# Reordering the first two batches of a linear-attention and bilinear-FFN kernel: kv before transposes in batch 0, x as full-row products in batch 1

## The chip, the cores and the metric

The kernel runs on one core of one Trainium2 chip. The metric is the device time of one execution in microseconds (us). One execution of each kernel was also taken with the hardware profiler. The profiled spans are about 1.8 us shorter than the times, because the span runs from the first to the last instruction.

In this text "PE" is TensorE, the matrix engine. "PEld" is its weight loads, "DVE" is VectorE, "ACT" is ScalarE and "POOL" is GpSimd. "SP" is the engine that issues the stores and the DMA transposes.

## The reference

```python
# q, k, v: (8 batches, 8 heads, 576 tokens, 64); g_norm: (64,)
kv  = einsum('bhsd,bhse->bhde', k, v)          # a 64x64 matrix per head
out = einsum('bhsd,bhde->bhse', q, kv)
rms = sqrt(mean(out * out, axis=-1) + 1e-6)
x   = (out / rms * g_norm)                     # as (4608 tokens, 512)
y   = ((x @ w_a) * (x @ w_b)) @ w_out          # 512 -> 1536 -> 512
```

## The kernel before

Heads are handled in pairs, so that two of 64 columns fill 128 partitions (the copies of `qT` in the trace are 128x576). For one pair the steps are as follows:

- transposes of q (`qtr`), then a DVE copy out of PSUM (`qtr_out`);
- kv (`kv1`), then a copy of it (`kv1_out`);
- x = q kv (`px`);
- squares on ACT (`psq`);
- sums of squares by a product with a block matrix of ones, then the reciprocal root on ACT (`pss`);
- the scaled result `xt` on DVE (`pst`).

`dummy` products of zeros fill PE's waits. The FFN works on strips of 512 tokens. Strip 0 needs batch 0 only, and strip 1 needs batch 1 too. Batches 0 and 1 are loaded and computed at the start. Later batches are computed between the FFN's products ("slots").

```python
        def px(self, p, i0):                 # x as four 64x64 products
            for h in range(2):
                for j in range(2):
                    r = slice(j * D, (j + 1) * D)
                    nc.tensor.matmul(P[r, i0 + h, 0:HF], lhsT=self.kvs[r, p, :],
                        rhs=self.qT[r, p, h * HF : (h + 1) * HF], start=True, stop=True)

        def x(self, p, i0):                  # x as two full-row products, kv block-diagonal
            for h in range(2):
                nc.tensor.matmul(P[:, i0 + h, 0:HF], lhsT=kvb[self.b % 2][:, p, :],
                    rhs=self.qT[:, p, h * HF : (h + 1) * HF], start=True, stop=True)
    # ... (cut) batch 0; banks of PSUM: X, SS = (4, 0), 6
    A.kv1(0, 3)
    A.kv1_out(0, 3, nc.vector.tensor_copy)
    for p in range(NP - 1):
        i = X[p % 2]
        A.qtr(p + 1, 2 + (p + 1) % 2)
        A.qtr_out(p + 1, 2 + (p + 1) % 2)
        if p:
            A.pst(p - 1, X[(p - 1) % 2])
        A.px(p, i)
        A.psq(p, i)
        # ... (cut) g_col at p == 0
        dummy(1, 2 + p % 2)
        A.kv1(p + 1, 2 + p % 2)
        dummy(1, 7)
        A.pss(p, SS)
        A.kv1_out(p + 1, 2 + p % 2, nc.vector.tensor_copy)
        if p < NP - 2:
            dummy(1, 2 + (p + 1) % 2)
    A.px(3, X[1])
    # ... (cut) squares of pair 3 in two halves, pst(2); the first two FFN units:
    u0.first((0, 1))                         # chunks 0 and 1 of w_a, then of w_b
    A.pss(3, SS, (0,))
    A.pst(3, X[1], (0,))
    u0.first((2,))                           # chunk 2: the "upper" weights
    A.pss(3, SS, (1,))
    A.pst(3, X[1], (1,))
    u1.first((0, 1, 2))
    u0.rest((3,))
```

## Time and profile before

| | before |
|---|---|
| median of 4 runs (range) | 323.93 us (323.7 to 324.06) |
| span of the profiled run | 322.1 us |
| PE busy | 97% of the span |
| granted PE clock | 1.000 |

The page of the kernel before, parts 1 and 4. Part 1 gives busy time per engine, and part 4 gives the chain of work that ended last, as shares of the span:

```profile
PE 314.1 (97%) x1922; PEld 151.0 (47%) x1957; DVE 124.3 (39%) x215; ACT 124.7 (39%) x212; POOL 60.3 (19%) x82
...
PE 87%; DMA 9%; POOL 1%; issue 1%; DVE 0%; ACT 0%; POOLq 0%; ACTq 0%
```

PE is the bound. Of the 9% of DMA in the chain, all but the last store (0.6%) lies in the first 33 us, where the first q and the weights arrive.

The view of waits of the kernel before, engine PE (who waited <- for whom: us in total, times, longest):

```profile
PE P L303 <- DVE eps_t L318: 1.2, 1, 1.2
PE P L137 <- issue: 0.5, 2, 0.3
PE P L161 <- DVE kvs L155: 0.3, 1, 0.3
PE P L278 <- issue: 0.3, 2, 0.2
PE P L234 <- DVE xt L202: 0.3, 1, 0.3
PE P L161 <- DVE qt L344: 0.2, 1, 0.2
```

PE's listed waits are 2.8 us in all, so almost everything left to save is work on PE itself.

The timeline of the kernel before, engine PE (start, us taken, what, count, and in brackets the idle time before it and what ended it). L137 is kv, L161 the transposes, L175 x as 64x64 products, L188 the sums, L234 the FFN's first layer, L278 its second:

```profile
7.12 0.38 PE L137 MATMUL P<-vt,kt 96*64 96x64 bf16 x12
7.82 0.45 PE L161 MATMUL P<-ident,qt 96*64 96x96 bf16 x12 [0.32 <-DVE kvs L155]
8.20 0.43 PE L175 MATMUL P<-qT,kvs 64*64 64x288 bf16 x4
...
14.42 0.43 PE L175 MATMUL P<-qT,kvs 64*64 64x288 bf16 x4
...
16.25 0.38 PE L234 MATMUL P<-xt,wa_t 128*128 128x512 bf16 x1 [0.31 <-DVE xt L202]
16.46 0.38 PE L234 MATMUL P<-xt,wb_t 128*128 128x512 bf16 x1
...
44.41 0.41 PE L188 MATMUL P<-sq,ones 128*128 128x288 bf16 x2
44.75 0.43 PE L175 MATMUL P<-qT,kvs 64*64 64x288 bf16 x4
45.11 0.45 PE L161 MATMUL P<-ident,qt 96*64 96x96 bf16 x12
```

At 7.82 us the transposes of pair 1 stand behind a DVE copy. At 14.42 us x of the last pair of batch 0 starts. Read distances between starts, because the durations of products overlap (the two at 16.25 and 16.46 us take 0.38 us each).

### The profile page before, as it was taken

How to read it: one execution, taken by the hardware profiler on the slowest of the kernel's cores; microseconds unless marked ns; L12 is line 12 of the kernel's file. 1: busy time of each engine (PE TensorE's matmuls, PEld its weight loads, DVE VectorE, ACT ScalarE, POOL GpSimd, SP SyncE). 2: the span in 40 equal slices, each digit the busy share in tenths (PEclk: the TensorE clock that was granted, in tenths of full speed). 3: DMA queues.
4: the chain of work that ended last, by engine and by line, in shares of the span. 5: the costliest groups of instructions: out<-in, count | busy, mean ns of one | idle time of the engine just before them, and what ended most of it. 6: DMA issues, size and time to landing. Idle time of an engine off the chain costs nothing.

```text
span 322.1 us, 4818 instructions
## 1 busy us (share of the span) xinstructions
PE 314.1 (97%) x1922; PEld 151.0 (47%) x1957; DVE 124.3 (39%) x215; ACT 124.7 (39%) x212; POOL 60.3 (19%) x82
## 2 busy tenths in 40 slices
PE   7999999999999999999999999999999999999995
PEld 3444454444444444444444445444444444444443
DVE  3544334344234433453244423532354243314421
ACT  3643245453335423552355325433453233123310
POOL 8855870330041240500050000000000000000000
PEclk9999999999999999999999999999999999999999
DMA  8999999795359899894598150003000200020002
GB/s 180 197 196 199 196 209 211 127 149 99 90 98 162 123 160 226 72 159 95 140 98 124 67 131 7 2 33 99 2 0 2 98 33 0 32 86 16 2 33 98
DMA packets 70043, 32.61 MB, mean 101 GB/s; under 512 B 43652, under 2 KB 65540, under 8 KB 70020
## 3 DMA queue, kind: packets, MB, share of 16 engines
q0 software_dynamic: 49712, 18.44, 48.5%
q1 hardware_dynamic: 19952, 13.50, 16.2%
q10 hardware_dynamic: 356, 0.36, 0.4%
q8 instruction: 15, 0.25, 0.3%
q14 instruction: 8, 0.07, 0.1%
HBM read 37.75 MB, written 12.98 MB: 157 GB/s over the span
## 4 chain that ended last, share of the span: by engine, by line
PE 87%; DMA 9%; POOL 1%; issue 1%; DVE 0%; ACT 0%; POOLq 0%; ACTq 0%
PE P L234 52%; PE P L278 28%; DMA wa_t<-in_moe_w_a_dram 5%; PE P L188 2%; PE P L214 2%; PE P L137 2%; DMA qt<-in_q_dram 2%; DMA wo_t<-in_moe_w_out_dram 1%; DMA out_dram<-osb 1%; PE P L161 0%; PE P L175 0%; POOL wb_t L108 0%; POOL wa_t L107 0%; POOL wa_t L331 0%; DVE osb L293 0%
## 5 line engine op out<-in xcount | busy, mean ns | idle before, releaser
L250 DVE TENSOR_TENSOR ab<-P,asb 128x512 bf16<-128x512 f32 x108 | 74.5, 692 | 124.0 <-PE P L234 123.1
L234 PE MATMUL P<-xt,wa_t 128*128 128x512 bf16 x425 | 111.4, 379 | 1.0 <-DVE xt L202 0.3
L234 PE MATMUL P<-xt,wb_t 128*128 128x512 bf16 x417 | 109.7, 379 | 0.4
L278 PE MATMUL P<-wo_t,ab 128*128 128x512 bf16 (+1 forms) x433 | 97.0, 373 | 0.8 <-issue 0.3
L248 ACT CAST asb<-P 128x512 bf16<-128x512 f32 x108 | 63.0, 585 | 81.5 <-PE P L234 80.0
L234 PEld LDWEIGHTS <-wb_t 128*128 128x128 bf16 x432 | 42.2, 98 | 51.2 <-DMA wb_t<-in_moe_w_b_dram 0.3
L278 PEld LDWEIGHTS <-ab 128*128 128x128 bf16 x444 | 43.0, 98 | 45.8 <-issue 0.2
L234 PEld LDWEIGHTS <-wa_t 128*128 128x128 bf16 x432 | 41.7, 98 | 44.5 <-DMA wa_t<-in_moe_w_a_dram 0.3
L202 DVE SCALAR_TENSOR_TENSOR xt<-P,g_col,rs 128x288 bf16<-128x288 f32 x64 | 30.2, 513 | 25.4 <-ACT rs L192 25.4
L192 ACT ACTIVATE rs<-P,eps_t 128x576 f32<-128x576 f32 (+1 forms) x33 | 24.0, 727 | 23.1 <-PE P L188 19.1
L291 ACT COPY osb<-P 128x512 f32<-128x512 f32 x17 | 10.0, 585 | 48.9 <-PE P L278 47.1
L184 ACT ACTIVATE sq<-P 128x576 bf16<-128x576 f32 x31 | 20.2, 650 | 20.3 <-PE P L214 18.0
L293 DVE COPY osb<-P 128x512 f32<-128x512 f32 x18 | 12.4, 691 | 32.5 <-PE P L278 32.5
L119 POOL DMA_DIRECT2D qs<-in_q_dram x12 | 19.6, 1633 | 1.7 <-issue 1.7
L116 POOL COPY gate<-qT 1x1 bf16<-1x1 bf16 x5 | 0.9, 176 | 92.7 <-DMA qT<-qs 92.7
L188 PE MATMUL P<-sq,ones 128*128 128x288 bf16 x64 | 13.2, 286 | 0.0
L214 PE MATMUL P<-qT,kvb 128*128 128x288 bf16 x48 | 10.0, 286 | 0.0
L188 PEld LDWEIGHTS <-ones 128*128 128x128 bf16 x64 | 6.3, 98 | 7.2
L96 POOL DMA_DIRECT2D vt<-in_v_dram x13 | 9.1, 702 | 1.1 <-DMA wo_t<-in_moe_w_out_dram 0.7
L96 POOL DMA_DIRECT2D kt<-in_k_dram x13 | 9.2, 709 | 0.0
L137 PE MATMUL P<-vt,kt 96*64 96x64 bf16 x384 | 8.6, 197 | 0.5 <-issue 0.5
L137 PEld LDWEIGHTS <-kt 96*64 96x64 bf16 x384 | 7.2, 112 | 3.6 <-issue 3.2
(43 smaller groups left out, 65.4 us busy)
## 6 DMA issues: line engine op xcount, KB each, us to landing
out_dram<-osb SPq DMA_DIRECT2D x23, 256.0 KB, 2.0
qs<-in_q_dram POOLq DMA_DIRECT2D x12, 288.0 KB, 6.7
kt<-in_k_dram POOLq DMA_DIRECT2D x6, 576.0 KB, 8.8
vt<-in_v_dram POOLq DMA_DIRECT2D x6, 576.0 KB, 11.1
out_dram<-osb SPq DMA_DIRECT2D x13, 128.0 KB, 2.3
wo_t<-in_moe_w_out_dram POOLq DMA_DIRECT2D x12, 128.0 KB, 6.3
wa_t<-in_moe_w_a_dram POOLq DMA_DIRECT2D x5, 256.0 KB, 9.2
wb_t<-in_moe_w_b_dram POOLq DMA_DIRECT2D x5, 256.0 KB, 9.8
```

The costliest lines, as they stand in the source:

```text
L96: nc.gpsimd.dma_start(out=t[:, hs, :, :], in_=src[b, hs].rearrange("h (t c) d -> t h c d", c=EC))
L119: nc.gpsimd.dma_start(out=d[:, hs, :], in_=q[b, hs].rearrange("h t d -> t h d"))
L137: nc.tensor.matmul(o[j * D : (j + 1) * D, :], lhsT=kt[self.b % NB][:, 2 * p + j, c, :], rhs=vt[self.b % NB][:, 2 * p + j, c, :], start=(c ...
L184: nc.scalar.activation(sq[p % 3], P[:, i0 : i0 + 2, 0:HF], AF.Square)
L188: nc.tensor.matmul(P[:, i0 + h, 0:HF], lhsT=ones, rhs=sq[p % 3][:, h, :], start=True, stop=True)
L192: nc.scalar.activation(rs[p % 3][:, h0:h1, :], P[:, i0 + h0 : i0 + h1, 0:HF], AF.Abs_reciprocal_sqrt, bias=eps_t,)
L202: nc.vector.scalar_tensor_tensor(out=xt[p][:, t0 : t0 + HF], in0=P[:, x0 + h, 0:HF], scalar=g_col, in1=rs[p % 3][:, h, :], op0=ALU.mult, o ...
L214: nc.tensor.matmul(P[:, i0 + h, 0:HF], lhsT=kvb[self.b % 2][:, p, :], rhs=self.qT[:, p, h * HF : (h + 1) * HF], start=True, stop=True,)
L234: nc.tensor.matmul(self.a if w is wa_t else self.b, lhsT=w[:, kc, self.fc * 128 : (self.fc + 1) * 128], rhs=xt[kc][:, t0 : t0 + STRIP], st ...
L248: nc.scalar.copy(self.t, self.a)
L250: nc.vector.tensor_mul(abt[self.s % 2][self.fc], self.b, self.t)
L278: nc.tensor.matmul(P[:, i, e0:e1], lhsT=abt[s % 2][fc][:, g * 128 : (g + 1) * 128], rhs=wo_t[:, fc, e0:e1], start=(fc == 0), stop=(fc == F ...
```

## The change

Its intent in batch 0 is to run kv as soon as its pair has landed, then the sums of squares of the pair before, then the next transposes, then x. The dummies stand in two places only, one product before the transposes and two behind x. Pair 0's kv uses a PSUM bank that the next transposes don't need. In batch 1, x runs as two full-row products (`x`) instead of four 64x64 ones (`px`), which needs two ACT copies per pair to fill the block diagonal.

```diff
-        def kv_out(self, src):
+        def kv_out(self, ps, src):
             for j in range(2):
                 r = slice(j * D, (j + 1) * D)
-                nc.scalar.copy(kvb[self.b % 2][r, :, r], src[r])
+                nc.scalar.copy(kvb[self.b % 2][r, ps, r], src[r])
 # ... (cut) batch 0: the loop shown above is replaced by
+    A.kv1(0, SS)
+    A.kv1_out(0, SS, nc.vector.tensor_copy)
+    A.qtr(1, 3)
+    A.qtr_out(1, 3)
+    A.px(0, X[0])
+    A.psq(0, X[0])
+    for p in range(1, NP):
+        i = X[p % 2]
+        A.kv1(p, 3 - p % 2)
+        A.kv1_out(p, 3 - p % 2, nc.vector.tensor_copy)
+        A.pss(p - 1, SS)
+        if p < NP - 1:
+            # ... (cut) g_col at p == 1
+            dummy(1, 2 + p % 2)
+            A.qtr(p + 1, 3 - p % 2)
+            A.qtr_out(p + 1, 3 - p % 2)
+            A.pst(p - 1, X[(p - 1) % 2])
+            A.px(p, i)
+            A.psq(p, i)
+            dummy(2, 2 + p % 2)
 # ... (cut) batch 1
-            A.px(n - 1, X[(n - 1) % 2])
+            A.x(n - 1, X[(n - 1) % 2])
 # ... (cut)
-            A.kv1_out(n, 2, nc.scalar.copy)
+            A.kv_out(n, P[:, 2, STRIP - D :])
 # ... (cut) the later batches' call of kv_out, with slice(0, NP) for all pairs
```

More of the change, by code (lines that the diff above doesn't have):

```diff
@@ L351 @@
     dummy(4, 7)
-    A.kv1(0, 3)
-    A.kv1_out(0, 3, nc.vector.tensor_copy)
-    for p in range(NP - 1):
-        i = X[p % 2]
-        A.qtr(p + 1, 2 + (p + 1) % 2)
-        A.qtr_out(p + 1, 2 + (p + 1) % 2)
-        if p:
-            A.pst(p - 1, X[(p - 1) % 2])
-        A.px(p, i)
-        A.psq(p, i)
-        if p == 0:
-            nc.tensor.matmul(P[:, 1, 0:1], lhsT=g_row, rhs=one, start=True, stop=True)
-            nc.vector.tensor_copy(g_col, P[:, 1, 0:1])
-        dummy(1, 2 + p % 2)
-        A.kv1(p + 1, 2 + p % 2)
-        dummy(1, 7)
-        A.pss(p, SS)
-        A.kv1_out(p + 1, 2 + p % 2, nc.vector.tensor_copy)
-        if p < NP - 2:
-            dummy(1, 2 + (p + 1) % 2)
+    A.kv1(0, SS)
[5 more added lines that the diff above has]
+    for p in range(1, NP):
+        i = X[p % 2]
+        A.kv1(p, 3 - p % 2)
+        A.kv1_out(p, 3 - p % 2, nc.vector.tensor_copy)
+        A.pss(p - 1, SS)
+        if p < NP - 1:
+            if p == 1:
+                nc.tensor.matmul(P[:, 1, 0:1], lhsT=g_row, rhs=one, start=True, stop=True)
+                nc.vector.tensor_copy(g_col, P[:, 1, 0:1])
+            dummy(1, 2 + p % 2)
+            A.qtr(p + 1, 3 - p % 2)
+            A.qtr_out(p + 1, 3 - p % 2)
+            A.pst(p - 1, X[(p - 1) % 2])
+            A.px(p, i)
+            A.psq(p, i)
+            dummy(2, 2 + p % 2)
     A.px(3, X[1])
@@ L427, in slot @@
             if n == k0 + kn - 1:
-                A.kv_out(kb)
+                A.kv_out(slice(0, NP), kb)
         for p in range(NP):
```

## The prediction

> **What bounds the kernel now.** TensorE. It is busy 97% of 322.1 us (page, part 1), and the view of waits lists 2.8 us for PE, all before 52 us. So what the change saves there should reach the end almost whole.
>
> **Batch 0 (5.8 to 18 us).** The timeline shows a TensorE-serial loop of 2.15 us a pair: transposes 0.38, x 0.36, kv 0.31, sums 0.25, three dummy products 0.85 with their tiling changes. One wait at the start: transposes of pair 1 stand 0.32 us behind the DVE copy of kv (7.76 us), because both use PSUM bank 3. At the end x(3) waits 0.28 us for its kv copy, which stands behind two 0.47 us DVE products. The change puts kv(0) into another bank, so transposes start at about 7.35 instead of 7.82 and x(0) at 7.82 instead of 8.20. The new loop also has three dummies, 2.12 us a pair by the same durations. Played through with them, x(3) starts at about 14.0 instead of 14.42, and xt of pair 2 ends at 15.7 instead of 16.19.
>
> That gain of 0.4 us meets DMA: the first-column chunks of w_a and w_b for the upper half land at 15.79 and 16.24 us (landings in the trace), whatever compute does. The second product on that w_b chunk starts at 16.46 now and can't start before about 16.28. So about **0.18 us** of the 0.4 survives. Later chunks land 0.7 us or more ahead of their use.
>
> **Batch 1 (40 to 52 us).** x as 4 products of 64x64 costs 0.36 us a pair, plus 0.1 to enter the tiled mode: a tiled product starts 309 ns after a 512-column one, where a full one starts after 216. [...]Full-row x is two products of 122 ns each (L214's and L188's spacing), directly behind the sums. Saved: 0.12 us at pairs 0, 1, 2 and 0.215 at pair 3, together **0.57 us**. Added: a second ScalarE copy of 64x64 a pair (about 0.2 us), which also delays the transposes' DVE copy by that much. qT of pair 2 then ends just before x(2) needs it (slack about 0.05 us), so up to 0.1 us may be lost.
>
> **Sum.** 0.18 + 0.57 - 0.03 = about 0.72 us: 323.92 to **323.2 us**, range 322.7 to 323.7 (the three runs before spread 0.36 us). Faster by over 2%: 0.005; within 2%: 0.985; slower by over 2%: 0.01.
>
> **Right or wrong in the profile.** Right: transposes of pair 1 directly behind kv(0); x(3) of batch 0 near 14.0; the first upper-half products waiting for w_a, then w_b DMA, at 15.8 and 16.3; from 17 us on everything 0.15 to 0.2 us earlier; at 52 us 0.7 to 0.8 us earlier; this lead constant to the end.
>
> **What would make it wrong.** [...](2) DMA landings shift with the stores. kv of batch 2 starts 0.9 us after its v has landed (59.59 us); with a 0.75 us lead the slack is 0.2. (3) A PSUM-bank wait that I missed, where transposes now share the bank with the kv just before them. (4) DVE order: kv copies behind the xt products.

The sum came to 0.18 + 0.57 - 0.03 = about 0.72 us.

## More of the kernel before

At 44.41 to 45.11 us, in batch 1, the sums and x take 0.70 us together.

## The result, and the profile after

The kernel after took 323.38 us (median of 4 runs, 323.22 to 323.68), beside 323.93 us (4 runs, 323.7 to 324.06). That is within the predicted range of 322.7 to 323.7. The ratio is 0.9985, with a 95% interval of 0.9968 to 1.0002. All ratios here are the mean time of one kernel's fast runs over that of the other's of the same rounds, so they are not quite the ratio of the medians quoted.

The difference is small, and the profiled execution of the kernel after was its slowest run (323.68 us). So it has to be read for where time went, not for how much was gained.

The page of the kernel after, parts 1 and 4:

```profile
PE 313.7 (97%) x1912; PEld 151.1 (47%) x1947; DVE 124.0 (39%) x215; ACT 125.3 (39%) x216; POOL 60.3 (19%) x82
...
PE 79%; DMA 14%; POOL 4%; issue 1%; DVE 0%; ACT 0%; POOLq 0%; ACTq 0%
```

Busy times hardly moved. The share of DMA in the chain rose from 9% to 14%, but that is no measure of waiting: a second profile of this same kernel (e1, below) has 3% there. The chain is followed back through whatever released each step last, and can take another path from run to run.

From the view of waits of the kernel after, engine PE:

```profile
PE P L303 <- DVE eps_t L318: 1.2, 1, 1.2
PE P L234 <- DMA wa_t<-in_moe_w_a_dram: 0.5, 1, 0.5
PE P L137 <- DMA vt<-in_v_dram: 0.3, 2, 0.2
...
PE P L188 <- ACT sq L184: 0.2, 1, 0.2
```

Both DMA waits are new, and so is the wait of the sums for ACT's squares. The waits for the DVE copies of kv (L161) and of `xt` (L234) are gone.

The timeline of the kernel after, engine PE. The lines answer to those shown of before; L214 is x as full-row products:

```profile
7.13 0.38 PE L137 MATMUL P<-vt,kt 96*64 96x64 bf16 x12
7.34 0.42 PE L161 MATMUL P<-ident,qt 96*64 96x96 bf16 x12
7.83 0.43 PE L175 MATMUL P<-qT,kvs 64*64 64x288 bf16 x4
8.43 0.38 PE L137 MATMUL P<-vt,kt 96*64 96x64 bf16 x12 [0.16 <-DMA vt<-in_v_dram]
9.01 0.41 PE L188 MATMUL P<-sq,ones 128*128 128x288 bf16 x2 [0.20 <-ACT sq L184]
...
14.11 0.43 PE L175 MATMUL P<-qT,kvs 64*64 64x288 bf16 x4
...
16.10 0.39 PE L234 MATMUL P<-xt,wa_t 128*128 128x512 bf16 x1 [0.47 <-DMA wa_t<-in_moe_w_a_dram]
16.57 0.39 PE L234 MATMUL P<-xt,wb_t 128*128 128x512 bf16 x1
...
44.41 0.41 PE L188 MATMUL P<-sq,ones 128*128 128x288 bf16 x2
44.65 0.41 PE L214 MATMUL P<-qT,kvb 128*128 128x288 bf16 x2
44.99 0.45 PE L161 MATMUL P<-ident,qt 96*64 96x96 bf16 x12
...
60.30 0.95 PE L137 MATMUL P<-vt,kt 96*64 96x64 bf16 x48 [0.16 <-DMA vt<-in_v_dram]
```

The PE side did what the durations say. The transposes of pair 1 stand directly behind kv. x of pair 3 starts 0.31 us earlier (14.11 for 14.42). In batch 1 the sums and x take 0.58 us instead of 0.70 (44.41 to 44.99 and to 45.11). But PE waits for transfers: for v of batch 0's pair 1 at 8.43 us, for w_a's upper chunk at 16.10 us, for w_b's at 16.57 us, and for v of batch 2 at 60.30 us.

To follow this, take one number at a time: the **lead**, the time at which a given weight load starts in the profile of before minus that time in another profile. In the profile after, the lead is 0.31 us at 14.8 us, -0.11 us at 18 us, 0.46 us at 52 us, and 0.23 us from 63 us to the end. So batch 0's gain was lost, and 0.11 us more, because w_b's upper chunk landed 0.28 us later than in the profile of before (16.52 for 16.24 us). Batch 1's 0.57 us (0.46 + 0.11) came whole, and 0.23 us were given back at batch 2's kv.

### The profile page after: what moved, and what is told of

Same layout as the page of the kernel before. It is cut to its first block, busy times and chain, and to the rows that moved or that the text cites. A ratio compares the mean times of both kernels' runs of the same rounds, so it can differ in the third digit from the quotient of the medians.

```text
span 321.9 us, 4806 instructions
## 1 busy us (share of the span) xinstructions
PE 313.7 (97%) x1912; PEld 151.1 (47%) x1947; DVE 124.0 (39%) x215; ACT 125.3 (39%) x216; POOL 60.3 (19%) x82
## 4 chain that ended last, share of the span: by engine, by line
PE 79%; DMA 14%; POOL 4%; issue 1%; DVE 0%; ACT 0%; POOLq 0%; ACTq 0%
PE P L234 49%; PE P L278 25%; DMA wa_t<-in_moe_w_a_dram 5%; DMA vt<-in_v_dram 4%; DMA wo_t<-in_moe_w_out_dram 2%; PE P L214 2%; PE P L188 2%; DMA qt<-in_q_dram 2%; PE P L137 2%; POOL qs L119 1%; POOL vt L96 1%; POOL kt L96 1%; DMA out_dram<-osb 1%; POOL qt L96 1%; POOL wa_t L331 0%
## 5 line engine op out<-in xcount | busy, mean ns | idle before, releaser
L234 PE MATMUL P<-xt,wa_t 128*128 128x512 bf16 x422 | 111.1, 379 | 1.4 <-DMA wa_t<-in_moe_w_a_dram 0.5
L234 PE MATMUL P<-xt,wb_t 128*128 128x512 bf16 x419 | 110.0, 379 | 0.4
L234 PEld LDWEIGHTS <-wb_t 128*128 128x128 bf16 x432 | 42.3, 98 | 51.2 <-DMA wb_t<-in_moe_w_b_dram 0.4
L234 PEld LDWEIGHTS <-wa_t 128*128 128x128 bf16 x432 | 41.7, 98 | 45.0 <-DMA wa_t<-in_moe_w_a_dram 0.9
L214 PE MATMUL P<-qT,kvb 128*128 128x288 bf16 x56 | 11.7, 286 | 0.0
L148 ACT CAST kvb<-P 64x256 bf16<-64x256 f32 (+1 forms) x20 | 6.0, 301 | 12.0 <-PE P L137 11.9
```

Source lines behind the costliest of these rows:

```text
L234: nc.tensor.matmul(self.a if w is wa_t else self.b, lhsT=w[:, kc, self.fc * 128 : (self.fc + 1) * 128], rhs=xt[kc][:, t0 : t0 + STRIP], st ...
```

## The experiments

The theory is that PE's work before 60 us shrank as costed, but each step may start only when its transfer has landed (in the profile after, w_b's upper chunk at 16.52 us and its product at 16.57 us). There are three such walls: the upper chunks of w_a and w_b (16 us), v of batch 1's pairs 2 and 3 (45 and 47 us), and v of batch 2 (60 us). (The profiles show a smaller fourth, v of batch 0's own pairs, at 8 to 13 us.) The lead at the end is what the tightest wall leaves.

The rival is that TensorE's own order bounds the start, and that the small result is noise or some other wait.

The table gives, for every profile, when the last of the 16 pieces of a transfer had arrived (from the landings in the trace) and the lead. Its second column has the starts of kv of pair 0 and of x of pair 3, both in batch 0. The lead is read at the first w_a load of FFN unit 2 (18 us), at the first of strip 1 (52 us), and at one at 87 us (after that it stays within 0.02 us).

| profile of | kv of pair 0, x of pair 3 | w_b upper | lead at 18 | v of pairs 2, 3 | lead at 52 | v of batch 2 | lead at end | time of this run |
|---|---|---|---|---|---|---|---|---|
| before | 7.12, 14.42 | 16.24 | 0 | 44.65, 47.10 | 0 | 59.59 | 0 | 323.94 |
| after | 7.13, 14.11 | 16.52 | -0.11 | 45.10, 47.43 | 0.46 | 60.26 | 0.23 | 323.68 |
| after, 2nd (e1) | 6.91, 13.88 | 16.28 | 0.12 | 44.52, 47.07 | 0.70 | 59.53 | 0.70 | 323.23 |
| after, 3rd (e10) | 7.15, 14.12 | 16.48 | -0.08 | 45.01, 47.36 | 0.50 | 60.13 | 0.36 | 323.54 |
| batch 0 only (e2) | 6.88, 13.85 | 15.77 | 0.57 | 44.91, 47.69 | 0.21 | 59.26 | 0.21 | 323.71 |
| batch 1 only (e3) | 7.16, 14.46 | 15.91 | -0.04 | 44.34, 46.89 | 0.54 | 59.26 | 0.54 | 323.37 |
| kv of batch 2 later (e4) | 6.89, 13.90 | 16.29 | 0.11 | 45.28, 47.95 | 0.17 | 60.12 | 0.16 | 323.76 |
| sums first (e5) | 7.14, 14.12 | 16.35 | 0.69 | 45.85, 48.76 | -0.64 | 60.28 | -0.64 | 324.55 |
| stores late (e6) | 6.86, 13.83 | 16.23 | 0.18 | 44.10, 46.32 | 0.75 | 57.28 | 0.75 | 323.18 |
| sums first, stores late (e7) | 7.52, 14.49 | 16.48 | 0.31 | 44.20, 46.41 | 0.89 | 56.46 | 0.89 | 323.04 |
| no upper wait (e8) | 7.21, 14.19 | 16.35 | 0.23 | 45.02, 47.29 | 0.64 | 59.77 | 0.64 | 323.26 |
| more PE instructions (e9) | 7.61, 14.86 | 16.18 | -0.45 | 44.14, 47.13 | 0.12 | 59.44 | 0.12 | 323.79 |
| as e7, again (e11) | 7.12, 14.10 | 16.28 | 0.71 | 44.44, 46.68 | 1.05 | 57.24 | 1.06 | 322.85 |
| no loop dummies (e12) | 6.75, 13.35 | 16.12 | 0.29 | 44.62, 46.90 | 0.87 | 59.45 | 0.87 | 323.03 |

Four things can be read at once. First, 323.94 us less the lead at the end gives the time of each profiled run to within 0.04 us, so the lead accounts for the time, and nothing after 87 us adds to it. Second, where no v was late (after, e1, e3, e6, e7, e9, e10, e12), the lead between 18 and 52 us changes by the same 0.57 or 0.58 us, which is batch 1's gain.

Third, the lead also contains how early a run began. Up to kv of pair 0 PE does the same in all these kernels but e9, yet that kv started anywhere from 6.75 to 7.52 us. From there to x of pair 3 PE took 7.30 us in both profiles with the old order (before, e3) and 6.97 to 7.01 us in all ten with the new order and its dummies, e9 apart. So the new order itself is worth 0.29 to 0.33 us, and the rest of any lead at x of pair 3 is the start of that run. Fourth, in the six profiles whose third products waited for the upper chunks (after, e1, e4, e6, e10, e12), the landing of w_b's upper chunk and the lead at 18 us add up to 16.40 or 16.41 us, however early x of pair 3 came. There the landing alone sets the lead.

### e1 and e10: the kernel after, again

These have no edit. They are on two other chips.

> The kernel after, unchanged, for a second profile and more timed rounds. If the first profile after was a run with late transfers (its first q landed 0.17 us and all weights 0.28 us later than in the profile before, although nothing of the change had run by then), this profile shows other landings: w_b's upper chunk anywhere from 16.2 to 16.6 us, and the lead at 18 us follows it one to one, between -0.15 and +0.2 us. If instead the change itself delays the transfers, the chunk lands at 16.5 us again. Time: 0.4 to 0.7 us below the kernel before.

> The kernel after, unchanged, as the partner on the same chip for the next two runs and a third profile. Lead over the profile before at 18 us: -0.12 to 0.57 us by when w_b's upper chunk lands; 0.57 us more by 53 us unless v of pair 2 or 3 lands too late; time 323.0 to 323.7 us.

e1 took 323.28 us (5 runs) beside 324.24 (9 runs), ratio 0.9972 (0.9960 to 0.9985). e10 took 323.16 us (5 runs) beside 324.13 (10 runs), ratio 0.9972 (0.9960 to 0.9985). So the gain is about 0.9 us there, and both intervals leave out 1. One of the ten runs of before in e10's rounds took 325.7 us and is in its mean.

The landings differ from run to run of one program: w_b's upper chunk arrived at 16.52, 16.28 and 16.48 us, and the lead at 18 us was -0.11, 0.12 and -0.08 us. No delay of the transfers by the change is seen: e2, with the same batch 0, had the chunk at 15.77 us. But with the old order there are two profiles only (16.24 and 15.91 us), which can't rule out a small one. e1's profile is the prediction almost to the letter: 0.12, then 0.70 us, kept to the end. That its chunk landed within 0.04 us of the 16.24 us that the prediction had taken is luck.

### e2 and e3: one part of the change alone

```diff
 e2 (from after): batch 1 back to
+            A.px(n - 1, X[(n - 1) % 2])
+            A.kv1_out(n, 2, nc.scalar.copy)
 e3 (from before): batch 1 with
+            A.x(n - 1, X[(n - 1) % 2])
+            A.kv_out(n, P[:, 2, STRIP - D :])
```

> The batch 0 part alone. Theory (its gain ends at a wait for the weights' transfer): x of pair 3 starts 0.3 us earlier (14.1 us), the products on the upper weight chunks wait for the transfers at about 16.1 and 16.5 us, the lead at 18 us is between -0.15 and +0.2 us, and so is the gain of the whole. Rival (TensorE alone bounds batch 0): lead of 0.3 us at 18 us, and 0.3 us less in time.

> The batch 1 part alone. Theory: the lead grows by 0.57 us between 40 and 53 us exactly as the durations say, but kv of batch 2 then waits for its v (it would start at 59.96 us; v landed at 59.6 in one trace and 60.26 in the other), so 0.25 to 0.57 us reach the end. Rival (all of batch 1's gain reaches the end): 0.57 us less, no wait at 60 us.

Beside 324.24 us of before, e2 took 323.84 us (ratio 0.9988, 0.9975 to 1.0000) and e3 323.77 us (0.9982, 0.9969 to 0.9994). The two differences of the medians, 0.40 and 0.47 us, add up to 0.87 us, near the whole's 0.96 us in the same rounds. At these intervals no interaction can be seen.

The expectation for e2 missed at 18 us, and usefully. In that run w_b's upper chunk had landed by 15.77 us, the third product waited only for `xt`, and the lead was 0.57 us instead of 0.2 at most. From the timeline of e2, engine PE:

```profile
6.88 0.38 PE L137 MATMUL P<-vt,kt 96*64 96x64 bf16 x12
...
13.85 0.43 PE L175 MATMUL P<-qT,kvs 64*64 64x288 bf16 x4
```

Of the 0.57 us, 0.24 us were there before anything of the change had run (kv of pair 0 at 6.88 for 7.12 us). The order gave the other 0.33 us, and without the wall all of it reached 18 us.

The gain was then lost at the next wall. The timeline of e2, engine PE, at the transposes and kv of pair 3 in batch 1:

```profile
47.27 0.45 PE L161 MATMUL P<-ident,qt 96*64 96x96 bf16 x12
47.73 0.38 PE L137 MATMUL P<-vt,kt 96*64 96x64 bf16 x12
```

kv follows its transposes after 0.46 us, where it takes 0.28 us without a wait (44.99 to 45.27 us in the profile after). Its v had landed at 47.69 us, 0.04 us before. Pair 2's kv followed after 0.41 us (44.95 us), 0.04 us behind its v, and so did e8's (45.06 us, v at 45.02 us). The view of waits lists nothing here, because the waiting product's gap is hidden behind the modelled end of the transposes. Only the distance of the starts and the landing show it.

In e3 the lead grew from -0.04 to 0.54 us and stayed, because v of batch 2 landed at 59.26 us in that run.

### e4: kv of batch 2 one unit later

```diff
-        k0, kn, xs = (4, 1, (6, 9, 11, 13)) if s < 3 else ...
+        k0, kn, xs = (4 + (s == 1), 1, (6, 9, 11, 13)) if s < 3 else ...
```

> The kernel after with kv of batch 2 one unit (1.73 us) later, so that its v has landed. Theory: no wait before kv of batch 2, and the lead that it had at 57 us is there to the end: 0.1 to 0.3 us less than the kernel after of the same rounds. Rival (the wait only moves, to the transposed q or to the kv copies before the first x of batch 2, which now has 1 unit instead of 2): no gain, and a gap at the first full-row x of batch 2 near 64.5 us.

e4 took 323.47 us (ratio 0.9975, 0.9962 to 0.9989), beside e1's 323.28 us on the same chip. There is no gain, so the expectation missed. The profile shows no gap at the first full-row x of batch 2 either. In that run v of pair 3 landed at 47.95 us and had already cut the lead to 0.17 us, at which kv of batch 2 would not have waited. The run neither proves nor refutes the 60 us wall. It shows that the walls stand in series, and that moving one step away from one of them is worth nothing when another is tighter.

### e8: no need for the upper chunk (wrong)

```diff
-                    lhsT=w[:, kc, ...],
+                    lhsT=w[:, 1 if self.s == 0 and self.fc < 2 and kc == 2 else kc, ...],
```

> Wrong on purpose: the first two units of strip 0 read the lower weight chunk (index 1) in place of the upper one's index 2, so they wait for the upper chunk of index 3 only, later. Everything else as in the kernel after. Theory (the wait for the upper chunks is what cuts batch 0's gain): the third products start at 15.6 to 16.0 us, behind xt of pair 2, not at the landing of w_a, and the lead at 18 us is 0.3 to 0.6 us however late the upper chunks land, as long as that is before 17 us. Rival: lead as in the kernel after, 0.1 us, with another wait in its place.

This is one run of unknown state, with a wrong result as intended (relative error 0.13). The timeline of e8, engine PE:

```profile
14.19 0.43 PE L175 MATMUL P<-qT,kvs 64*64 64x288 bf16 x4
...
16.02 0.38 PE L234 MATMUL P<-xt,wa_t 128*128 128x512 bf16 x1 [0.31 <-DVE xt L202]
16.23 0.38 PE L234 MATMUL P<-xt,wb_t 128*128 128x512 bf16 x1
```

The chunks landed late in this run too (15.87 and 16.35 us), yet the third products start behind `xt`, 0.21 us apart. x of pair 3 led by 0.23 us (14.42 less 14.19), and the lead at 18 us is the same 0.23 us. In the profile after, 0.31 us went in at x of pair 3 and -0.11 us came out. Taking the wait away keeps the gain. It is somewhat below the 0.3 to 0.6 us expected, because this run began later (kv of pair 0 at 7.21 us, 0.09 us behind before); the order's 0.32 us are whole.

### e9: the late piece of the upper chunks, and a packet of the instruction queue

In the profile of before, fifteen of the 16 pieces of w_b's upper chunk had arrived by 15.34 us and the last at 16.24 us, 0.90 us later. For w_a's upper chunk it was 1.13 us (14.66 and 15.79 us). The same trace has one packet of 16,384 bytes of the instruction queue that starts at 13.59 us and took 0.945 us; PE has 263 records (products and weight loads) before it.

The theory was that this packet comes by the number of instructions that PE has run, and that it is what makes the piece late. The kernel e9 makes PE run 56 more instructions (28 products and their weight loads) over the same number of columns:

```diff
-    dummy(11, 0)
+    dummy(4, 0)
+    dummy(32, 0, 64)
+    dummy(3, 0)
```

> The kernel after with 28 more dummy products at the start, in the same time (four of 512 columns replaced by 32 of 64), so that TensorE has run 56 more instructions by any later point. In every profile so far one 16 KB packet of the instruction queue (0.94 us) falls at 13.5 to 14.3 us[...]. Theory[...]: the packet comes 1 to 3 us earlier (10.5 to 12.5 us), and the late piece appears first on a chunk before w_a's upper one, on v of pair 3 or on w_a's lower chunk. Rival (the packet comes at a fixed time, or something else paces it): it stays at 13.5 to 13.9 us.

The packet came at 12.07 us (13.83 us in the profile after), and the late piece appeared three transfers earlier, on v of pair 3 (the fourth transfer, w_b lower, is left out here). Arrivals of the last two of the 16 pieces, from the landings:

```
                 v of pair 3       w_a lower        w_a upper        w_b upper
before           12.54, 12.63      13.20, 13.33     14.66, 15.79     15.34, 16.24
e9               12.56, 14.12      13.27, 14.31     14.59, 15.48     15.27, 16.18
e2               12.58, 12.59      13.30, 13.31     14.62, 14.63     15.30, 15.77
```

The next packet of 16,384 bytes moved as well, to 27.64 us from 32.2 to 33.9 us in the other profiles. In all 14 profiles PE's records number 263 to 277 at the first packet and 449 to 456 at the second, 174 to 190 more. So these two packets go with PE's instruction count and not with the time. After the first packet, one piece of each transfer in the table is late in before and e9. In e2 w_a's upper chunk has no late piece (14.62 and 14.63 us) and w_b's one of 0.47 us; why is not shown. That the packet is what delays the piece is not shown either: it rests on their times alone.

In e9 kv of pair 3 waited 0.21 us for its v, whose last piece landed at 14.12 us. The full clock also came on late there (6.71 us), so its total of 323.79 us says nothing about the packet alone.

### e12: without the loop's dummies

```diff
-            dummy(1, 2 + p % 2)
-            dummy(2, 2 + p % 2)
```

> The kernel after without the six dummy products in batch 0's loop. Theory: by the durations the loop takes 1.9 us a pair instead of 2.14 us, so x of pair 3 starts 0.3 to 0.6 us earlier than in the kernel after (13.5 to 13.8 us), and nothing of it reaches 18 us, because the same upper weight chunks are waited for; time as the kernel after.[...]

e12 took 323.21 us (4 runs, ratio 0.9975, 0.9962 to 0.9989), beside e10's 323.16 us on the same chip. The timeline of e12, engine PE:

```profile
13.35 0.43 PE L175 MATMUL P<-qT,kvs 64*64 64x288 bf16 x4
...
15.69 0.39 PE L234 MATMUL P<-xt,wa_t 128*128 128x512 bf16 x1 [0.82 <-DMA wa_t<-in_moe_w_a_dram]
16.16 0.39 PE L234 MATMUL P<-xt,wb_t 128*128 128x512 bf16 x1
```

x of pair 3 came 0.76 us earlier than in the profile after, and the wait for w_a grew from 0.47 to 0.82 us. Half of the 0.76 us is the run's start (kv of pair 0 at 6.75 for 7.13 us); the missing dummies gave 0.38 us. Kv of pairs 1, 2 and 3 now waited 0.32, 0.38 and 0.59 us for their v, so the loads of batch 0's v are a wall as well. The lead at 18 us is 0.29 us, and the time is the same. The clock held without the dummies too (full from 4.57 us in the profile, mean 1.000). No cost and no use of the dummies is seen here; they fill the time in front of walls. Two of its four runs had a mean clock of 0.998, but so did three of five runs of e3, whose batch 0 is that of the kernel before. The profiled runs with a mean below 1 are those of e7 (0.999) and e9 (0.998).

### e5, e6, e7, e11: using the walls

e5 gives PE work that doesn't need the upper chunk while that is on its way, and moves the last sums to the front. e6 puts the stores of strip 0, which are issued from 39.74 us on in the profile of before, behind the loads of batch 1's k and v. e7 and e11 do both, and are the same kernel.

```diff
 e5:
     A.pss(3, SS, (0,))
     A.pst(3, X[1], (0,))
-    u0.first((2,))
     A.pss(3, SS, (1,))
     A.pst(3, X[1], (1,))
-    u1.first((0, 1, 2))
+    u1.first((0, 1))
+    u0.first((2,))
+    u1.first((2,))
 e6:
-        store(s * STRIP + g * 128, t, 0, d_model)
+        if s == 0:
+            held.append((g * 128, t))
+        else:
+            store(s * STRIP + g * 128, t, 0, d_model)
 ...                                  # in strip 1's loop, behind transpose_q(2)
+            if s == 1 and n == 5:
+                for t0, t in held:
+                    store(t0, t, 0, d_model)
```

> The kernel after, with the end of batch 0 reordered: both halves of pair 3's sums of squares before anything that needs the upper weight chunks, then the products on the lower chunks of both units, then the upper ones. By the durations of the profile after, the first product on xt of pair 3 moves from 18.2 to about 17.4 us, and the lead at 18 us grows by 0.6 to 0.8 us whether or not the upper chunk is late. Theory (transfers are the wall of the first 60 us): the lead is then cut back by v of batch 1's pairs (landed 44.5 to 45.3 and 46.9 to 47.95 us in the five profiles so far) and of batch 2 (59.3 to 60.3 us), so that at most 0.4 us of it, on average 0.2 us, is there at the end: 0.1 to 0.4 us less than the kernel after. Rival (only TensorE's order counts): 0.6 us less or more, no waits for v.

> The kernel after, with the stores of strip 0 (0.79 MB written between 40 and 57 us) put behind the transpose of batch 2's q[...]. Theory: v of pairs 2 and 3 lands 0.5 to 2 us earlier than 44.5 and 46.9 us, no wait in batch 1, and the spread of the times narrows; 0 to 0.3 us less than the kernel after. It may land v of batch 2 or its transposed q later; a wait at 60 or 65 us would show that. Rival (the stores don't matter for these landings): landings as before.

> Both of the two edits, as the version that should beat both kernels. If the stores hold back v: lead of 1.0 to 1.4 us at 53 us over the kernel before, and what of it is left after kv of batch 2 (v landed at 59.3 to 60.3 us where it would be needed at 59.2) is 0.5 to 1.2 us: 322.9 to 323.7 us beside 324.24 us of the kernel before. If not, as the run with the sums first alone.

> Sums first and stores late, unchanged from the earlier run, beside the kernel after on one chip. Theory: 0.2 to 0.6 us below the kernel after of the same rounds (322.7 to 323.2 us); in the profile, v of pairs 2 and 3 lands by 44.3 and 46.5 us, v of batch 2 by 57.5 us, no wait on any of them. In its first profile the full clock came on at 6.4 us, later than in all others (3.9 to 5.3 us); with an earlier one the lead at 18 us should be 0.7 us instead of 0.31 us, and 1.2 us from 53 us on.

With the stores late, v lands earlier (e6, e7 and e11 in the table): v of pair 3 at 46.32 to 46.68 us instead of 46.89 us or later, and v of batch 2 at 56.46 to 57.28 us instead of 59.26 to 60.28 us. How the stores hold the loads back is not shown. The stores of strip 0 are 512 rows of 2,048 bytes, 1.05 MB by the trace, not the 0.79 MB of the expectation for e6. All runs are beside 324.06 us of before (11 runs), except e11, which is beside 324.13 us (10 runs).

- **e5** took 323.65 us (6 runs, 322.88 to 324.55; ratio 0.9986, 0.9972 to 1.0000). It gained the 0.69 us at 18 us and lost it again, where 0 to 0.4 us had been expected to stay. Its stores began at 39.05 us (39.74 before), and v of pairs 2 and 3 landed at 45.85 and 48.76 us, later than in any other profile. The timeline of e5, engine PE:

```profile
45.89 0.38 PE L137 MATMUL P<-vt,kt 96*64 96x64 bf16 x12 [1.17 <-DMA vt<-in_v_dram]
...
48.80 0.38 PE L137 MATMUL P<-vt,kt 96*64 96x64 bf16 x12 [0.27 <-DMA vt<-in_v_dram]
```

  The profiled run was the slowest of six, and the fastest was 1.67 us below it. A wall of varying height would give such a spread, but only one of the six was profiled.

- **e6** took 323.19 us (0.9972, 0.9959 to 0.9985). v of pairs 2 and 3 landed at 44.10 and 46.32 us, v of batch 2 at 57.28 us (59.3 to 60.3 us in all profiles with early stores), and no kv of batches 1 and 2 waited. The spread did not narrow as expected (323.02 to 323.72 us).

- **e7** took 323.00 us (5 runs; 0.9963, 0.9951 to 0.9975). **e11** took 322.88 us (5 runs, 322.82 to 323.08; 0.9964, 0.9950 to 0.9977), beside 323.16 us of the kernel after in the same rounds (e10). The difference to e10 is 0.28 us, and the two intervals overlap. No DMA wait is left in its view of waits. The timeline of e11, engine PE, where the third products and the first on pair 3's `xt` stand:

```profile
16.54 0.38 PE L234 MATMUL P<-xt,wa_t 128*128 128x512 bf16 x1
16.75 0.38 PE L234 MATMUL P<-xt,wb_t 128*128 128x512 bf16 x1
...
17.40 0.38 PE L234 MATMUL P<-xt,wa_t 128*128 128x512 bf16 x1
```

  The first product on pair 3's `xt` starts at 17.40 us (18.11 before, 18.22 after). The lead is 0.71 us at 18 us, 1.05 us at 52 us and 1.06 us at the end. Of batch 1's 0.57 us, 0.23 us are missing: kv of pairs 0 and 1 now started at 39.95 and 42.20 us, each 0.04 us after its v had landed (39.91 and 42.16 us), so the next wall is in sight. e11 has the lowest median, and its result is correct.

## Why the prediction was right or wrong, point by point

- **The bound, and the size of the whole: right.** Predicted were 323.2 us and 0.72 us saved. Measured were 323.38, 323.28 and 323.16 us (medians of three sets), which is 0.55, 0.96 and 0.97 us below the kernel before of the same rounds. The first set alone doesn't show a gain (its interval reaches 1.0002), and that the sum came so near is partly luck: in the three profiles the parts were -0.11 to 0.12 us for batch 0, 0.57 or 0.58 us for batch 1, and 0 to 0.23 us given back.
- **Batch 1, 0.57 us: right in mechanism and size.** In all three profiles of the kernel after, and in e3, the lead grew by 0.57 or 0.58 us. The costing was by spacing: 216 ns from one 512-column product to the next, 309 ns where a tiled one follows (93 ns more), and 122 ns for 288 columns. The traces of before and after show 215 to 216, 309, and 122 to 123 ns. The second ACT copy was feared to cost up to 0.1 us and was booked at 0.03 us; it cost nothing.
- **Batch 0's order: right in place, somewhat large in size.** Transposes at 7.34 us and x of pair 0 at 7.83 us were predicted as 7.35 and 7.82. x of pair 3 was predicted at 14.0 and stood at 14.11 and 13.88 us (after, e1). But e1's whole run was early by 0.21 us (kv of pair 0 at 6.91 us). Counted from kv of pair 0, the order was worth 0.29 to 0.33 us in the ten profiles, not 0.42 (14.42 less 14.0). The prediction had no wait for ACT's squares in the new loop; in the profile after the sums of pair 0 waited 0.20 us for them at 9.01 us. That this is the missing 0.1 us is not shown.
- **Batch 0's surviving 0.18 us: the right wall, but not one number.** The term took the landing of w_b's upper chunk in one profile, 16.24 us, as fixed. It varied from 15.77 to 16.52 us, and the lead at 18 us with it: -0.11, 0.12 and -0.08 us in the three profiles of the kernel after. For the landing that it assumed, the arithmetic was right: 16.41 less 16.24 is 0.17 us. By time, batch 0 alone gave 0.40 us (e2). The difference between these readings is not settled. There is one profile of the kernel before, of a run of 323.94 us, and its medians on the other chips were 324.06 to 324.24 us. The kernel before may lose time at these walls too, which no profile here shows.
- **"This lead constant to the end": not always.** In the profile after, 0.23 us were given back at batch 2's kv, whose v landed at 60.26 us; 0.14 us in e10 and none in e1. The prediction named this under what could go wrong (slack of 0.2 us), but didn't book it. It didn't name v of batch 1's pairs 2 and 3, which cost 0.36 us in e2 (0.57 to 0.21) and 1.9 us in e5 (0.69 + 0.57 in hand, -0.64 left).
- **The clock: no loss.** The full clock came on between 3.8 and 5.3 us in all but two profiles (6.42 us in e7, 6.71 us in e9) and in the profiles of before and after it held past PE's last product (to 322.37 and 322.28 us; the products start at 318.27 and 318.05 us). The mean is 1.000 in all three profiles of the kernel after, and without the loop's dummies too (e12). Before it came on, 512-column products started 426 to 427 ns apart in the profile of before, and 216 ns apart after it. The spread is not small: with the same first products the full clock came on at 3.85 to 6.42 us, and in the run with the latest (e7) kv of pair 0 started at 7.52 us instead of 7.12, and the lead at 18 us was 0.31 us instead of e11's 0.71 us for the same kernel.
- **A PSUM-bank wait or the DVE order: only as before.** x of pair 3 still waits 0.28 us for its kv copy, behind two `pst` products, as it did before.

## What to carry to other kernels

Before you price a saving in the first part of a kernel, list when each transfer lands and when its first reader needs it. What you save in front of the tightest landing only lengthens a wait (e12: 0.76 us earlier, nothing gained). The landing and the start of a run both differ by some tenths of a us from run to run (w_b's upper chunk at 15.77 to 16.52 us, kv of pair 0 at 6.75 to 7.52 us without e9). So measure a reordering from a point before which nothing was changed (here kv of pair 0), and remember that one profile of each kernel can't settle a change of this size.

To move a wall, look for traffic that can wait. Postponing the stores of strip 0 brought v of batch 2 forward by 2.0 to 3.8 us and v of batch 1's pair 3 by 0.2 us or more. Only then was a better order on PE kept to the end in the profiles (lead of -0.64 us in e5, 1.06 us in e11). By time the better order is 0.19 us on top of the late stores (e7 beside e6 in the same rounds), with overlapping intervals.
